# Cosine attention and a hard-swish feed-forward on one core: a new hand-written order of all engines' work, first products that may be issued in two pieces, and other blocks of zero products early on

## The chip, the cores and the metric

The program runs on one core of one Trainium2 chip. The time is the device time of one launch, in microseconds (us), and smaller is better. The kernel before the change took 399.28 us (median of three runs, 398.77 to 400.17).

A core has a matrix engine (TensorE; PE in the profile, its weight loads are PEld), three engines for elementwise work (VectorE is DVE, ScalarE is ACT, GpSimd is POOL), and a queue engine (SyncE, SP) that does nothing here but issue DMA transfers. Each engine takes its instructions strictly in program order and waits, where it must, for semaphores that other engines set.

## The reference

```python
q_n = q / (norm(q, axis=-1) + 1e-06)              # q, k, v: 8 x 12 x 448 x 64
k_n = k / (norm(k, axis=-1) + 1e-06)
attn = softmax(q_n @ k_n.T / tau)                 # tau = 0.1
x = (attn @ v).transpose(0, 2, 1, 3).reshape(8 * 448, 768)
h = x @ w_in                                      # 768 x 2048
g = h * clip(h + 3.0, 0.0, 6.0) / 6.0
out = g @ w_out                                   # 2048 x 768
```

## The kernel before

Heads are worked on in pairs: 8 batches of 12 heads make 48 "items" `i`, six to a batch. Query and key come in as separate loads, so that `j` counts 0 to 47 over them: `j` = 2d and 2d + 1 are query and key of items 2d and 2d + 1.

All engines' order comes from one list of short words, `PLAN` (lines 19 to 117), that `run` (near the end of the file) reads from left to right. Each word issues the instructions of one step, and each engine gets its instructions in the order in which their words stand there. Nothing is rearranged later. The words that matter here:

- `LQ.j` loads 448 KB of query or key through SP's queue (line 262), `LV.d` loads values (line 271). `SQ.j.e.c.n` squares columns c to c + n on engine e (a is ACT, line 296; v is DVE and p is POOL, line 298). `RE.j` sums them (DVE, line 310). `NO.d` makes the reciprocal norms for two j, four short ACT instructions (lines 326 to 329). `NM.j.e` multiplies (line 341); a last number means one of the two heads only.
- `TR.j.Y` or `TR.j.Z` transposes on PE (line 398), for the first 14 j; after them `XD.j` does it by a DMA on SP's queue (line 409). `CQ.i`, `CK.i` and `CS.i` copy the transposed pieces out of PSUM (lines 418 and 420).
- `SC.i.g` is the scores of item i in four groups g (PE, lines 499 and 502), `EX.i.g` their exponentials (ACT, line 521), `VC.i` casts the values (lines 361 and 363), `VA.i.g` multiplies by them into the accumulator `PV` (PE, line 537), `FI.i` divides by the sum (DVE, lines 557 and 558). `BK.i` and `CX.i` transpose the result back into `xT` and copy it (line 575, line 420); `XB` and `XP` do so by DMA.
- `F.b.c` is one first product of batch b, six matmuls over the six chunks of `xT` (PE, line 671); `FA` and `FV` are its two activation steps (ACT line 680, DVE line 686). It needs the results of all six items of its batch. `G` and `P` are the sums and products of the second matrix (line 812, line 837), `BO`, `RS`, `PE.` their combination.
- `W.n` is one of ten weight loads, issued by POOL (line 1131). `DP.n` issues n products of zeros on PE (line 1142) into a part of `PV` that nobody reads; their zeros are `xT` of the second batch, set by DVE at line 1185.

For the first six items the scores go through two PSUM buffers `SC`, and `SC.i.g` waits until the exponentials two groups back have read its buffer. The word `OPEN` ends that: from item 6 on, the same memory is four of the six banks of one ring (M in the profile, with Y and Z), which scores, transposes, first and second products share in turn.

In the list before, the early `DP` blocks have 23, 16, 4, 3, 4, 2, 1 and 3 products, in that order; the first stands ahead of `TR.0`, the second ahead of `TR.1`, the one of 1 after `FI.0`, the last one between `FI.4` and `VA.5.0`.

Of the kernel before, what the change touches and what calls it, by code (L numbers as in the profile page):

```python
# [120 lines left out]
def kernel(  # L121
# [11 lines left out]
    B, H, S, D = q.shape  # L133
# [3 lines left out]
    HP = H // 2  # L137
# [498 lines left out]
    def g_of(b):  # L636
        return gT[b % 2]
# [17 lines left out]
    def g_left(b, e="v"):  # L655
# [3 lines left out]
        engines[e].tensor_copy(out=g_of(b + 1)[:, :, 0:SR], in_=g_of(b)[:, :, S - SR : S])  # L659
        left_done.add(b)  # L660

    def mm1_unit(b, fc):
        needs(*(("CX", i) for i in range(b * HP, (b + 1) * HP)))
        assert all({2 * n, 2 * n + 1} <= weights_in for n, c in enumerate(FF) if c <= 128 * fc)
        assert not any(x in "34" for x, _ in in_summed)
# [569 lines left out]
```

## Time and profile before

| | |
|---|---|
| time, median of three | 399.28 us (398.77 to 400.17) |
| profiled execution, its own time | 401.33 us |
| its span, first to last instruction | 399.5 us |
| mean granted TensorE clock | 0.989 |
| transfers | 64.87 MB, mean 162 GB/s |
| zero products | 56, 10.0 us of PE |

The span is that of one profiled execution. In a row of a timeline stand the start, the time that the instructions of the row took together, the engine, the line, the operation, out and in tiles, and how many; in brackets the idle time ahead of it and what ended it. A row of a window table has, for a stretch of the span, its length, each engine's busy time and count, the granted clock of PE (1.00 is full), and the DMA engines' share and rate. The busy share of the engines in forty equal slices shows at once that PE is full from the fourth slice on:

```profile
PE   4988999999999999999999999999999999999995
ACT  6896999989966888896756876888687567844420
PEclk9898999999999999999999999999999999999999
```

### The profile page before, as it was taken

To read this page: it belongs to the slowest core of one execution; us is meant where nothing else is said; L and a number is where in the kernel's file an instruction comes from. 1 tells how busy PE (TensorE), PEld (TensorE's weight loads), DVE (VectorE), ACT (ScalarE), POOL (GpSimd) and SP (SyncE) were. 2 spreads that over 40 slices of the span, in tenths; PEclk is the share of its full clock that TensorE was granted. 3 is DMA by queue.
4 is the path that set the end of the run, shared out by engine and by line. 5 is a ranking of instruction groups with operands and counts; after the bars stand their busy time and mean duration, and the time that the engine had idled before them with its cause. 6 is when DMAs were issued, how large, how long until landed. Compare 5 with 4: busy or idle time off the path is not lost.

```text
span 399.5 us, 10001 instructions
## 1 busy us (share of the span) xinstructions
PE 385.0 (96%) x3776; PEld 240.9 (60%) x3776; DVE 309.4 (77%) x545; ACT 295.6 (74%) x670; POOL 299.0 (75%) x269
## 2 busy tenths in 40 slices
PE   4988999999999999999999999999999999999995
PEld 3655556545655556655555556655666679977763
DVE  6797877998969698687766968854878868987862
ACT  6896999989966888896756876888687567844420
POOL 4999886799679946477838693778798989675752
PEclk9898999999999999999999999999999999999999
DMA  8979989997899987895996598765466350012124
GB/s 292 309 220 250 208 201 276 185 157 154 206 205 236 194 189 178 192 229 166 200 191 152 140 218 169 194 148 132 107 139 123 82 119 14 2 40 61 40 60 118
DMA packets 90239, 64.87 MB, mean 162 GB/s; under 512 B 55760, under 2 KB 89424, under 8 KB 90192
## 3 DMA queue, kind: packets, MB, share of 16 engines
q1 hardware_dynamic: 85280, 57.56, 59.3%
q0 software_dynamic: 4512, 6.29, 9.3%
q8 instruction: 29, 0.48, 0.5%
q10 hardware_dynamic: 400, 0.39, 0.3%
q14 instruction: 18, 0.15, 0.1%
HBM read 46.73 MB, written 11.01 MB: 145 GB/s over the span
## 4 chain that ended last, share of the span: by engine, by line
PE 81%; POOL 6%; ACT 3%; DVE 3%; DMA 3%; issue 2%; SPq 0%; POOLq 0%; DVEq 0%; ACTq 0%
PE M L837 16%; PE M L671 16%; PE PV L537 10%; PE V L837 6%; PE M L1026 6%; PE M L502 5%; PE Y L671 4%; PE Y L837 4%; PE Z L837 3%; PE Z L671 3%; DMA big<-in_k_dram 2%; POOL nrm L341 2%; ACT att L521 2%; PE Y L502 2%; PE Z L502 1%
## 5 line engine op out<-in xcount | busy, mean ns | idle before, releaser
L521 ACT ACTIVATE att<-M 128x448 bf16<-128x448 f32 x193 | 95.7, 560 | 14.7 <-PE M L502 13.1
L671 PE MATMUL M<-xT,w_in_sb 128*128 128x448 bf16 x396 | 82.9, 353 | 0.0
L671 PEld LDWEIGHTS <-w_in_sb 128*128 128x128 bf16 x576 | 53.1, 98 | 46.8 <-issue 3.4
L341 POOL TENSOR_TENSOR nrm<-big,r 128x896 bf16<-128x896 f32 (+1 forms) x36 | 61.7, 1720 | 16.6 <-ACT r L329 13.0
L537 PEld LDWEIGHTS <-att 128*128 128x128 bf16 (+1 forms) x1536 | 56.3, 97 | 22.7 <-issue 9.9
L537 PE MATMUL PV<-vx,att 128*128 128x65 bf16 (+1 forms) x1536 | 64.9, 194 | 0.0
L837 PEld LDWEIGHTS <-gT 128*128 128x128 bf16 x448 | 42.9, 98 | 28.7 <-POOL gT L812 1.4
L686 DVE SCALAR_TENSOR_TENSOR gT<-u,M 128x448 bf16<-128x448 bf16 x66 | 39.5, 616 | 18.6 <-ACT u L680 18.3
L310 DVE TENSOR_REDUCE n<-big 128x14 f32<-128x896 f32 (+1 forms) x50 | 51.5, 1042 | 1.6 <-ACT big L296 1.3
L680 ACT ACTIVATE u<-M 128x448 bf16<-128x448 f32 x66 | 35.8, 555 | 10.8 <-PE M L671 9.7
L298 POOL TENSOR_TENSOR big<-big 128x896 f32<-128x896 f32 (+2 forms) x19 | 31.5, 1657 | 13.2 <-DMA big<-in_k_dram 6.5
L837 PE MATMUL M<-w_out_sb,gT 128*128 128x384 bf16 x224 | 40.4, 326 | 0.7 <-POOL gT L812 0.7
L837 PEld LDWEIGHTS <-gs 128*128 128x128 bf16 x296 | 28.1, 98 | 18.8 <-issue 1.3
L812 POOL TENSOR_TENSOR gT<-gT 128x1024 bf16<-128x1024 bf16 x15 | 31.9, 2125 | 9.5 <-DVE gs L812 9.0
L558 DVE TENSOR_TENSOR on<-PV,rc 128x512 bf16<-128x512 f32 x48 | 33.2, 691 | 1.6
L837 PE MATMUL M<-w_sum,gs 128*128 128x384 bf16 (+1 forms) x192 | 34.0, 323 | 0.0
L502 PE MATMUL M<-tT,kz 64*128 64x448 bf16 (+1 forms) x171 | 33.4, 356 | 0.6 <-DVE gT L686 0.4
L868 POOL TENSOR_TENSOR big<-big 128x384 f32<-128x384 f32 x14 | 18.3, 1308 | 17.8 <-ACT big L625 15.0
L812 POOL TENSOR_TENSOR gs<-gT 128x1024 bf16<-128x1024 bf16 x14 | 29.7, 2126 | 2.3 <-DVE gT L686 1.2
L521 ACT ACTIVATE att<-Z 128x448 bf16<-128x448 f32 x51 | 28.5, 558 | 1.3 <-PE M L502 1.0
L521 ACT ACTIVATE att<-Y 128x448 bf16<-128x448 f32 x50 | 28.0, 560 | 1.5 <-PE Z L502 1.5
L458 POOL COPY km<-tT 64x128 bf16<-64x128 bf16 x34 | 16.4, 484 | 12.5 <-PE Y L502 5.1
(146 smaller groups left out, 758.9 us busy)
## 6 DMA issues: line engine op xcount, KB each, us to landing
big<-in_q_dram SPq DMA_DIRECT2D x24, 448.0 KB, 4.4
big<-in_k_dram SPq DMA_DIRECT2D x24, 448.0 KB, 4.4
out_dram<-o SPq DMA_DIRECT2D x107, 96.0 KB, 2.2
big<-in_v_dram SPq DMA_DIRECT2D x68, 128.0 KB, 3.2
big<-in_v_dram SPq DMA_DIRECT2D x7, 448.0 KB, 7.0
w_out_sb<-in_moe_w_out_dram POOLq DMA_DIRECT2D x4, 768.0 KB, 10.0
w_in_sb<-in_moe_w_in_dram POOLq DMA_DIRECT2D x4, 384.0 KB, 5.3
w_in_sb<-in_moe_w_in_dram POOLq DMA_DIRECT2D x2, 768.0 KB, 8.4
```

The costliest lines, as they stand in the source:

```text
L298: engines[e].tensor_tensor(out=o, in0=i, in1=i, op=ALU.mult)
L310: nc.vector.tensor_reduce(out=n2s[d % 2][:, j % 2, c], in_=sq[:, :, :, :].rearrange("p g c d -> p (g c) d")[:, c, :], axis=AX.X, op=ALU.add,)
L341: engines[e].tensor_tensor(out=nrm[:, :, g, :].rearrange("p c g d -> p g c d"), in0=raw_of[j][:, g, :, :], in1=rs[d % 2][3][:, j % 2, :] . ...
L502: nc.tensor.matmul(o, ks, qt[rows], start=True, stop=True)
L521: nc.scalar.activation(out=o, in_=x, func=AF.Exp, scale=inv_tau)
L537: nc.tensor.matmul(pv_out(j, h), at[rows, n, q_cols(i // HP, j)], vt[rows, 3 + h if name == "M" else 5 * h + int(name[1]), :], start=(name ...
L558: nc.vector.tensor_tensor(out=on[:, :, :, :].rearrange("p j h d -> p h j d"), in0=pv4[:, :, :, 0:D], in1=rc[:, :, :].to_broadcast([128, 2, ...
L671: nc.tensor.matmul(ps[:, 0:S], w_in_sb[:, cc, fc * 128 : (fc + 1) * 128], x[:, cc, 0:S], start=(cc == 0), stop=(cc == CC - 1),)
L680: nc.scalar.activation(out=u[:, :], in_=ps[:, 0:S], func=AF.Relu, bias=0.5, scale=1.0 / 6.0)
L686: nc.vector.scalar_tensor_tensor(out=g[:, fc, c0 : c0 + S], in0=u[:, :], scalar=1.0, in1=ps[:, 0:S], op0=ALU.min, op1=ALU.mult,)
L812: engines[e].tensor_tensor(out=o[:, :, :], in0=x, in1=y, op=op)
L837: nc.tensor.matmul(m, lhs[:, c, :], rhs[:, c, c0 : c0 + width], start=(base is None and c == 0), stop=(c == KC - 1), skip_group_check=True,)
```

## The change

Three things change; the arithmetic is the same, and each kind of instruction but the zero products keeps its count.

First, `PLAN` is another list, 1902 words for 1899. No block of it is the same for long: the order differs on every engine. Some of the words that name an engine name another one now; on balance ACT gets four squares more, POOL six casts of values more and ACT and DVE three fewer each, DVE both halves of the weight sum `IS.6` from POOL, and four copies of second products from ACT. Its first line in the list before and now:

```diff
-    "LQ.0 SQ.0.v.6.2 SQ.0.a.0.6 RE.0.0 SQ.0.a.8.6 RE.0.1 LQ.1 SQ.1.p.0.4 SQ.1.a.4.3 RE.1.0 SQ.1.v.11.3 SQ.1.a.7.4 RE.1.1 LQ.2 NO.0.0 SQ.2.a.0.7 LQ.3",
+    "LQ.0 SQ.0.a.6.2 SQ.0.a.8.6 SQ.0.v.0.6 RE.0.0 RE.0.1 NO.0.0 LQ.1 SQ.1.a.7.4 SQ.1.v.11.3 RE.1.1 SQ.1.a.4.3 SQ.1.p.0.4 RE.1.0 NM.0.v.1 LQ.2 SQ.2.a.0.7",
```

Second, the early zero blocks are 31, 16, 3, 7, 3, 8, 1 and 3 products, 72 in all. The first two stand ahead of `TR.0` and `TR.1` as before, the one of 1 after `FI.0`; the block between `FI.4` and `VA.5.0` is gone, and the last block of 3 stands ahead of `SC.2.1.1`.

Third, a first product can be issued in two pieces, and the list has three such, `FP.0.3.4`, `FP.0.2.4` and `FP.0.1.4` (the first four chunks), each with its `F.0.c` (the other two) some words later. All three stand behind `CX.5`, the copy of the last chunk of that batch.

```diff
-    def mm1_unit(b, fc):
-        needs(*(("CX", i) for i in range(b * HP, (b + 1) * HP)))
+    part_of = {}
+
+    def mm1_chunks(b, fc, ps, chunks):
+        needs(*(("CX", b * HP + cc) for cc in chunks))
...
+        for cc in chunks:
             nc.tensor.matmul(
                 ps[:, 0:S],
                 w_in_sb[:, cc, fc * 128 : (fc + 1) * 128],
-                x[:, cc, 0:S],
+                xT[b % 2][:, cc, 0:S],
                 start=(cc == 0),
                 stop=(cc == CC - 1),
             )
+
+    def mm1_part(b, fc, n):
+        ps, key = bank_of(None, 1)
+        narrow.discard(key)
+        mm1_chunks(b, fc, ps, range(n))
+        part_of[(b, fc)] = ps, key, n
+
+    def mm1_unit(b, fc):
+        firsts_read.add((b, fc))
+        g, c0 = g_of(b), b % 2 * SR
+        if (b, fc) in part_of:
+            ps, key, n = part_of.pop((b, fc))
+        else:
+            (ps, key), n = bank_of(None, 1), 0
+            narrow.discard(key)
+        mm1_chunks(b, fc, ps, range(n, CC))
```

What moves is seen at three places. On ACT, from the first square to the second group of norms (L296 are squares, L326 to L329 the four instructions of `NO`), it was

```order
L296 ACTIVATE big_87<-big_87 128x384 x2
L296 ACTIVATE big_87<-big_87 128x192
L296 ACTIVATE big_87<-big_87 128x256
L326 ACTIVATE ln0_94<-n20_92 128x14
L327 ACTIVATE nr0_95<-ln0_94 128x14
L328 ACTIVATE le0_96<-nr0_95 128x14
L329 ACTIVATE r0_97<-le0_96 128x14
L296 ACTIVATE big_87<-big_87 128x896
L326 ACTIVATE ln0_94<-n20_92 128x14
```

and now is

```order
L296 ACTIVATE big_87<-big_87 128x128
L296 ACTIVATE big_87<-big_87 128x384
L326 ACTIVATE ln0_94<-n20_92 128x14
L327 ACTIVATE nr0_95<-ln0_94 128x14
L328 ACTIVATE le0_96<-nr0_95 128x14
L329 ACTIVATE r0_97<-le0_96 128x14
L296 ACTIVATE big_87<-big_87 128x256
L296 ACTIVATE big_87<-big_87 128x192
L296 ACTIVATE big_87<-big_87 128x896
L326 ACTIVATE ln0_94<-n20_92 128x14
```

ACT's two squares of the first key load (192 and 256 wide) have moved behind the first group of norms; what ACT no longer squares of the first query load, DVE does.

On DVE, after the second and third sums of squares (`CK.0` is the first row of the first list, `FI.0` its L557 and L558), it was

```order
L420 COPY kz0_80<-Y_107 128x448
L310 TENSOR_REDUCE n20_92<-big_87 128x14 x2
L420 COPY kz1_81<-Y_107 128x448
L341 TENSOR_TENSOR nrm0_89<-big_87,r1_101 128x2x7x64
L361 TENSOR_REDUCE vx_88<-big_87 64x8x64 x2
L298 TENSOR_TENSOR big_87<-big_87 128x896
L420 COPY tT2_85<-Z_108 128x448
L557 RECIPROCAL rc_331<-PV_106 128x8
L558 TENSOR_TENSOR on_330<-PV_106,rc_331 128x2x4x64
L420 COPY kz0_80<-Y_107 128x448
L310 TENSOR_REDUCE n21_93<-big_87 128x14
```

and now is

```order
L420 COPY tT1_84<-Z_108 128x448 x2
L420 COPY kz0_80<-Y_107 128x448
L310 TENSOR_REDUCE n20_92<-big_87 128x14
L420 COPY kz1_81<-Y_107 128x448
L310 TENSOR_REDUCE n20_92<-big_87 128x14
L341 TENSOR_TENSOR nrm0_89<-big_87,r1_101 128x2x7x64
L298 TENSOR_TENSOR big_87<-big_87 128x896
L420 COPY tT2_85<-Z_108 128x448
L310 TENSOR_REDUCE n21_93<-big_87 128x14
L361 TENSOR_REDUCE vx_88<-big_87 64x8x64 x2
L420 COPY kz0_80<-Y_107 128x448
L557 RECIPROCAL rc_351<-PV_106 128x8
```

The two query copies are new on DVE (they were ACT's), and `RE.7` (the L310 that writes n21) and `CK.2` (the second copy into kz0) have moved ahead of `FI.0`.

On SP, where the DMA transposes begin (L262 are loads of query or key, L409 the transposes `XD`, L281 and L271 loads of values, L610 a transpose of results), it was

```order
L262 DMA big_87<-in_k_dram 128x2x448 x2
L262 DMA big_87<-in_q_dram 128x2x448 x2
L262 DMA big_87<-in_k_dram 128x2x448
L281 DMA big_87<-in_v_dram 64x2x256 x4
L409 DMA_TRANSPOSE tT2_85<-nrm0_89 128x7x128
L409 DMA_TRANSPOSE tT0_83<-nrm2_91 128x7x128
L262 DMA big_87<-in_q_dram 128x2x448
L409 DMA_TRANSPOSE tT0_83<-nrm1_90 128x7x128
```

and now is

```order
L409 DMA_TRANSPOSE tT0_83<-nrm2_91 128x7x128
L262 DMA big_87<-in_q_dram 128x2x448
L409 DMA_TRANSPOSE tT2_85<-nrm0_89 128x7x128
L409 DMA_TRANSPOSE tT0_83<-nrm1_90 128x7x128
L409 DMA_TRANSPOSE tT1_84<-nrm2_91 128x7x128
L262 DMA big_87<-in_k_dram 128x2x448
L610 DMA_TRANSPOSE xT0_69<-on_1463 128x8x128
```

The load `LQ.20`, second of the two loads in the first row before, now is the last but one row: it has moved behind the four transposes `XD.14` to `XD.17`.

More of the change, by code (lines that the diff above doesn't have):

```diff
@@ L660, in g_left @@
         left_done.add(b)
-    def mm1_unit(b, fc):
-        needs(*(("CX", i) for i in range(b * HP, (b + 1) * HP)))
+    part_of = {}
+    def mm1_chunks(b, fc, ps, chunks):
+        needs(*(("CX", b * HP + cc) for cc in chunks))
         assert all({2 * n, 2 * n + 1} <= weights_in for n, c in enumerate(FF) if c <= 128 * fc)
         assert not any(x in "34" for x, _ in in_summed)
-        firsts_read.add((b, fc))
-        x, g, c0 = xT[b % 2], g_of(b), b % 2 * SR
-        ps, key = bank_of(None, 1)
-        narrow.discard(key)
-        for cc in range(CC):
+        for cc in chunks:
             nc.tensor.matmul(
@@ L1160 @@
         "GL": g_left, "WS": lambda x, *h: weight_sums(str(x), *((h[0] * KC // 2, KC // 2) if h else (0, KC))), "D": busy, "DP": busy_pv, "OPEN": open_ring,
-        "F": mm1_unit, "S": single_unit, "G": lambda x, n, e="v": g_sum(n, str(x), e), "P": product, "TB": tail_banks, "WR": wide_ring,
+        "F": mm1_unit, "FP": mm1_part, "S": single_unit, "G": lambda x, n, e="v": g_sum(n, str(x), e), "P": product, "TB": tail_banks, "WR": wide_ring,
         "IS": lambda x, e, *n: in_sum(str(x), e, *n), "XS": lambda b, x, *e: x_sum(b, str(x), *e), "QA": quad_first, "QB": quad_second, "QC": quad_third,
```

192 rows, old and new, of the table PLAN are left out of this document.

## The prediction

> **What bounds the kernel now.** I read the page's shares first, then the span in windows, then PE's waits, then the timeline of the first 40 us.
>
> ```profile
> PE 385.0 (96%) x3776; PEld 240.9 (60%) x3776; DVE 309.4 (77%) x545; ACT 295.6 (74%) x670; POOL 299.0 (75%) x269
> PE 81%; POOL 6%; ACT 3%; DVE 3%; DMA 3%; issue 2%; SPq 0%; POOLq 0%; DVEq 0%; ACTq 0%
> ```
>
> PE is busy 385.0 of 399.5 us and makes 81% of the chain that ended last. The share hides that the limits differ by stage, so I cut the span where the work changes: at the first zero product, the first transpose, the first exponential, the end of the fourth group of norms, the first first-product, and the last product.
>
> ```profile
> 2.50:9.18 6.68, 3.92 (x23) 2.87 (x24) 4.15 (x10) 4.17 (x14) 1.74 (x10) 0.96 1.03 384
> 9.18:14.10 4.92, 4.85 (x38) 3.67 (x38) 2.78 (x4) 3.30 (x8) 4.68 (x4) 0.71 1.06 381
> 14.10:35.86 21.76, 18.23 (x274) 12.01 (x273) 20.54 (x41) 20.92 (x37) 21.09 (x21) 1.00 0.89 218
> 35.86:42.56 6.70, 6.57 (x95) 4.42 (x95) 4.33 (x13) 4.11 (x10) 6.59 (x7) 0.75 0.98 351
> 42.56:395.60 353.04, 351.43 (x3350) 217.98 (x3348) 275.82 (x474) 261.85 (x603) 262.99 (x222) 1.00 0.67 150
> ```
>
> From 42.56 us on, PE is busy 351.43 of 353.04 us at full clock: 1.61 us of idle in nine tenths of the program. The list does not change what PE multiplies there, so that stage gets shorter by at most 1.61 us, and can get longer by any new wait. Up to 42.56 us PE is fed by others: from 14.10 to 35.86 ACT is busy 20.92 of 21.76 us, so ACT sets the pace, and before that a chain of loads, squares and norms does. So the question is when PE fills for good, now at 42.56 us, and whether it stays full.
>
> ```profile
> PE Z L398 <- DVE nrm L341: 2.7, 1, 2.7
> PE PV L1142 <- DVE on L558: 1.8, 2, 1.1
> PE M L837 <- POOL gT L812: 0.7, 1, 0.7
> ```
>
> PE's waits agree: 2.7 us ahead of `TR.0`, 1.8 us where zero products wait for `FI`, and one of 0.7 us late.
>
> **Up to the first exponential.** The rows of the chain:
>
> ```profile
> 4.55 0.94 ACT L296 ACTIVATE big<-big 128x384 f32<-128x384 f32 x2 [2.52 <-DMA big<-in_q_dram]
> 5.75 0.67 ACT L296 ACTIVATE big<-big 128x192 f32<-128x192 f32 x2 [0.27 <-DMA big<-in_k_dram]
> 6.33 0.20 ACT L326 ACTIVATE ln<-n 128x14 f32<-128x14 f32 x1
> 6.45 0.62 DVE L310 TENSOR_REDUCE n<-big 128x7 f32<-128x448 f32 x1 [0.20 <-ACT big L296]
> 7.17 0.93 ACT L296 ACTIVATE big<-big 128x896 f32<-128x896 f32 x1
> 8.09 0.21 ACT L326 ACTIVATE ln<-n 128x14 f32<-128x14 f32 x1
> 7.98 1.15 DVE L341 TENSOR_TENSOR nrm<-big,r 128x448 bf16<-128x448 f32 x2
> 9.04 2.07 DVE L310 TENSOR_REDUCE n<-big 128x14 f32<-128x896 f32 x2
> 9.12 1.84 POOL L341 TENSOR_TENSOR nrm<-big,r 128x448 bf16<-128x448 f32 x2 [2.70 <-ACT r L329]
> 9.18 0.93 PE L398 MATMUL Z<-ident,nrm 128*128 128x128 bf16 x7 [2.75 <-DVE nrm L341]
> 9.90 2.92 PE L1142 MATMUL PV<-xT 128*128 128x248 bf16 x16
> 12.66 0.55 PE L398 MATMUL Y<-ident,nrm 128*128 128x128 bf16 x7
> 13.05 0.59 PE L1142 MATMUL PV<-xT 128*128 128x248 bf16 x4
> 13.25 0.39 DVE L420 COPY kz<-Y 128x448 bf16<-128x448 bf16 x1 [2.14 <-PE Y L398]
> 14.10 2.97 ACT L521 ACTIVATE att<-SC 128x896 bf16<-128x896 f32 x4 [1.26 <-PE SC L502]
> ```
>
> The two parts of the first query's squares are dealt out the other way, and the sums still begin near 5.1 us; the first norms stay at 6.33 to 7.26. Behind them ACT now squares its part of the first key load (0.67 us, before done from 5.75), so `RE.1.1` starts at 7.6, `RE.1.0` ends at 8.8 (0.6 us each), and DVE's half of `NM.0` (1.15 / 2), queued behind both, ends at 9.35. `TR.0` starts at 9.4 instead of 9.18. POOL's half, 0.92 us from 7.3, lies beside. The second norms start at 8.85 instead of 8.09, `NM.1` on POOL ends at 11.7 instead of 10.96.
>
> Before, that slack of `NM.1` was worth nothing, because 16 zero products stood between the two transposes at half clock: 2.92 us. At full clock the block of 4 shows about 0.11 us apart, so 16 take 1.7. `TR.0` 9.4 to 9.95, zeros to 11.65, `TR.1` 11.75 to 12.3, if the clock holds. On DVE, `RE.2` and `RE.3` now end near 11.9 (`SQ.3` on ACT ends at 10.75 behind the norms), the two query copies at 12.65, `CK.0` at 13.05. In the old trace the first exponential follows the start of `CK.0` by 0.85 us; less its 0.39 us, that is 0.45 behind its end: 13.5. So it comes 0.6 us earlier. The eight more zeros of the first block (0.11 to 0.17 us each) end at 7.4, inside the 2.75 us of idle: they cost nothing up to that gap's length.
>
> **The clock.** Whether it holds is the largest doubt here:
>
> ```profile
> 5.24:8.65 3.41, 1.20 (x11) 0.86 (x9) 3.10 (x7) 2.98 (x11) 0.61 (x1) 1.00 1.04 387
> 8.67:12.06 3.39, 2.88 (x18) 2.32 (x19) 2.44 (x3) 3.03 (x8) 2.70 (x3) 0.50 1.06 382
> 32.56:35.95 3.39, 1.91 (x24) 1.20 (x21) 2.40 (x9) 2.79 (x7) 3.20 (x4) 1.00 0.98 191
> 35.97:39.37 3.40, 3.38 (x40) 2.32 (x40) 1.51 (x7) 0.98 (x2) 3.40 (x3) 0.50 1.03 361
> ```
>
> Twice a stretch of 3.4 us at half clock follows one in which PE was busy 1.20 and 1.91 us. The changed first block leaves PE idle from 7.4 to 9.4, 2.0 us, so a stretch that holds all of it has 1.4 us of work: between the two. If it halves again, `TR.1` is at 13.2 and the first exponential at 14.65. The Trainium skill ("TensorE: Matmul & The Clock Gate", "Part 1: The HAM clock gate") says that such stretches run free, so that their phase differs from run to run, and that at least one idle stretch throttles. The trace doesn't agree with the second: after 1.91 us of work in 3.39 the clock was already halved. By that rule of the Trainium skill alone no gap of 2.0 us could halve the clock, and rival 1 below would fall away.
>
> **From the first exponential to the ring.**
>
> ```profile
> 18.24 1.36 DVE L298 TENSOR_TENSOR big<-big 128x896 f32<-128x896 f32 x1
> 20.06 0.69 DVE L558 TENSOR_TENSOR on<-PV,rc 128x512 bf16<-128x512 f32 x1
> 20.67 0.38 DVE L420 COPY kz<-Y 128x448 bf16<-128x448 bf16 x1
> 20.96 1.08 DVE L310 TENSOR_REDUCE n<-big 128x14 f32<-128x896 f32 x1
> 21.16 3.41 ACT L521 ACTIVATE att<-SC 128x448 bf16<-128x448 f32 x5
> 35.63 0.23 ACT L329 ACTIVATE r<-le 128x28 f32<-128x28 f32 x1
> 35.99 0.78 PE L1142 MATMUL PV<-xT 128*128 128x248 bf16 x3 [1.12 <-DVE on L558]
> 38.16 0.98 ACT L521 ACTIVATE att<-M 128x448 bf16<-128x448 f32 x2 [2.30 <-PE M L502]
> ```
>
> The zero product behind `FI.0` still stands ahead of `SC.2.0.0`, and `FI.0` is now queued behind `RE.7` and `CK.2` on DVE. From the end of `CK.0` (13.6) to that of `FI.0` (20.75) DVE took 7.15 us; with 1.0 and 0.3 more, and from 13.05, it is 21.5. `EX.2.0` can start near 22.05. ACT would be ready at 13.5 + 7.6 = 21.1 (before, 14.10 to 21.70 with the same instructions): a new gap of 1.0 us, and 0.35 us behind the old trace. Bounds: 0, if DVE's queue runs closer, and 1.3, all that was put ahead of `FI.0`.
>
> From there ACT did 13.8 us of work up to 35.86, the end of `NO.4`, and then idled 2.30 us for the first scores of the ring. The list puts `NO.4` ahead of `EX.5.2`, so that gap is filled: ACT has the same 13.8 us, plus some 0.6 us of small gaps where a score stands behind `VA` on PE (0 to 1.2), and reaches the ring at 36.45. `SC.6.0` needs only the buffer that `EX.5.2` frees 0.55 us earlier, and the copies of `TR.7`, which PE now does near 35. So `EX.6.0` comes near 36.5 instead of 38.16: 1.65 us earlier. Of that, the zero block behind `FI.4`, gone with its wait of 1.1 us, and the half clock from 35.97 are what made the old ring late; what is late next is `FI.5`. `VA.6.2` (0.25 us) now stands behind the first first-products, so 1.4 us remain when PE fills.
>
> The other zeros (7 and 8, 1.7 us) stand ahead of scores that wait for ACT's 0.8 us exponentials; without that cover they'd cost those 1.7 us. The `FP` pieces add no matmul and each stands behind the copy of the last chunk, so their early start is never used: zero. The last products are the same, and so is the end.
>
> **The full stage.** I take the old 1.6 us of waits, bounds 0 and 4.5. Below: PE cannot idle less than nothing. Above: POOL's longest wait for a load, where a square is placed close behind its load, is
>
> ```profile
> 205.53 1.68 POOL L298 TENSOR_TENSOR big<-big 128x896 f32<-128x896 f32 x1 [4.24 <-DMA big<-in_k_dram]
> big<-in_k_dram SPq DMA_DIRECT2D x24, 448.0 KB, 4.4
> 42.63 1.24 PE M L671 x6
> ```
>
> 4.24 us, of which 0.7 us reached PE. I take the middle of nothing new, since 0.7 is the nearest thing that this stage has shown.
>
> **The sum.** 399.5 - 1.4 = 398.1 us of span. The profiled execution took 401.33 us in its own count and the median is 399.28; I carry the difference over: 399.28 - 1.4 = 397.9 us.
>
> **Rivals.** (1) *The gain is eaten at the start.* The clock halves at `TR.0` again: the first exponential at 14.65 shifts DVE's queue and all behind it by 1.15 us, leaving 0.25: 399.0 us. For it, the row with 1.20 us; against it, eight more zeros.
>
> (2) *Slower: ACT stands still at `SQ.20`.* `LQ.20` is now behind `XD.17` on SP, and `SQ.20` is on ACT as the next word, with `EX.16.1` and the activations of two first-products behind. `XD.17` waits for `SC.13.3`. Between that and `SQ.20` PE has six first-products (1.14 us apart), nine score groups (0.2) and eight value groups (0.3), some 11 us, against 4.4 us for the load and the issue of transposes. That speaks against it. If the transposes hold SP back until PE has reached `SC.16.0`, ACT waits 4.4 us more; PE covers two first-products of it, 2.3, and idles 2.1 us, and as much again where DVE and the ring follow late: 4.2 - 1.4 = 2.8 us slower, 402.1, or 400.5 with the first wait alone and the start's gain lost by half. I say 401. It decides from a landing over 2.3 us behind `SQ.20`'s turn.
>
> (3) *More than hoped.* `FI.0` is in time and the late waits go: 397.9 - 1.0 - 0.7 = 396.2.
>
> **How the numbers follow.** Forecast 0.48, rival 1 0.21, rival 2 with other new waits of PE in the full stage 0.24, rival 3 0.07. A measurement here tells about 0.3%, 1.2 us, from no change: faster is below 398.1, slower above 400.5. The forecast's own range, 396.9 to 399.3, gives 0.37 faster, 0.08 same, 0.03 slower; rival 1 gives 0.02, 0.14 and 0.05; rival 2 is slower, rival 3 faster. Together 0.46, 0.22 and 0.32. The range reaches from rival 3 to rival 2: 396.0 to 401.3; it leaves out the ends at which two bounds come together.
>
> **What would show it.** Right: PE's clock stays at full from 5 us on, the first exponential near 13.5, an ACT gap of about 1 us near 21 ended by a score, no gap of 2.3 us ahead of the first exponential out of M, the first first-product near 41, PE idle some 1.6 us from there on. Wrong: a window at 0.50 behind the first zero block (rival 1); a wait of ACT for a load by L296 near 90 us, or waits of PE over 3 us behind 42 us (rival 2). If the first first-product comes early and the time doesn't, the new order lost it in the full stage.

## The result and the profile after

The changed kernel takes 401.27 us (median of 20 runs, 399.08 to 403.49), the kernel before, run beside it, 398.95 us (20 runs, 397.44 to 400.80). The ratio is 1.0062, with a 95% interval of 1.0046 to 1.0077: slower by 2.3 us, where 1.4 us less were predicted. The two profiled executions lie only 1.1 us apart in span, because the one of before was a long one: 401.33 us, 2.4 above the median of its kernel, against 1.2 for the changed kernel's.

The profiled execution of the changed kernel took 402.48 us, its span is 400.6 us. First the page: busy time by engine, the chain that ended last by engine, and PE's busy tenths and clock in forty slices.

```profile
PE 385.8 (96%) x3792; PEld 243.4 (61%) x3792; DVE 308.8 (77%) x547; ACT 293.2 (73%) x663; POOL 295.5 (74%) x274
PE 83%; DVE 6%; ACT 5%; DMA 3%; POOL 2%; issue 1%; SPq 0%; ACTq 0%; DVEq 0%; POOLq 0%
PE   5887999999999999999999999999999999999995
PEclk9988999999999999999999999999999999999999
```

Little differs: PE is busy 0.8 us longer, with 16 more zero products. But in the chain DVE has 6% for 3% before, and PE's fourth slice (30 to 40 us) now shows 7 tenths. It showed 8 before, where PE was full from the fifth slice on. The windows say the same in numbers (columns as in the prediction's window table). The first two rows are the start, the last runs from the first first-product to where PE's work thins out at the end.

```profile
14.00:36.00 22.00, 18.23 (x235) 11.44 (x234) 19.23 (x32) 19.10 (x31) 19.89 (x20) 0.92 0.92 225
36.00:43.00 7.00, 6.30 (x95) 4.42 (x95) 5.68 (x17) 4.05 (x10) 5.68 (x5) 0.76 0.84 277
45.29:396.60 351.31, 350.55 (x3358) 219.62 (x3356) 272.44 (x474) 260.25 (x598) 259.87 (x228) 1.00 0.69 150
```

Behind the first first-product PE idles 0.76 us in 351.31, against 1.61 in the row of before: the long stage is better by 0.85 us. Ahead of it ACT, which set the pace with 20.92 of 21.76 us, is busy 19.10 of 22.00 us, and the first first-product starts at 45.29 instead of 42.56 us. From there on 355.3 us of the span remain instead of 356.9; of the difference 0.85 is idle time, the rest PE's work that now stands ahead of that point. So the start lost 2.7 us and the rest gave 1.6 back. Where the start lost them, in order of time (rows of the timelines of ACT, DVE, PE and POOL):

```profile
13.98 2.53 ACT L521 ACTIVATE att<-SC 128x896 bf16<-128x896 f32 x3 [0.43 <-PE SC L502]
21.43 0.69 DVE L558 TENSOR_TENSOR on<-PV,rc 128x512 bf16<-128x512 f32 x1
22.18 0.27 PE L1157 MATMUL PV<-xT 128*128 128x248 bf16 x1 [1.17 <-DVE on L558]
22.78 0.92 ACT L521 ACTIVATE att<-SC 128x896 bf16<-128x896 f32 x1 [1.19 <-PE SC L502]
26.24 0.21 DVE L557 RECIPROCAL rc<-PV 128x8 f32<-128x8 f32 x1 [2.53 <-PE PV L537]
27.88 0.23 ACT L329 ACTIVATE r<-le 128x28 f32<-128x28 f32 x1
28.24 1.69 POOL L341 TENSOR_TENSOR nrm<-big,r 128x896 bf16<-128x896 f32 x1 [0.97 <-POOL vx L363]
29.87 1.35 POOL L1146 DMA_DIRECT2D w_in_sb<-in_moe_w_in_dram  x2
30.90 2.99 DVE L298 TENSOR_TENSOR big<-big 128x896 f32<-128x896 f32 x1
31.23 1.71 POOL L341 TENSOR_TENSOR nrm<-big,r 128x896 bf16<-128x896 f32 x1
35.63 0.69 DVE L558 TENSOR_TENSOR on<-PV,rc 128x512 bf16<-128x512 f32 x1
36.38 0.60 PE L537 MATMUL PV<-vx,att 128*128 128x65 bf16 x8 [1.77 <-DVE on L558]
37.35 0.23 ACT L326 ACTIVATE ln<-n 128x28 f32<-128x28 f32 x1 [1.37 <-DVE n L310]
41.19 0.98 ACT L521 ACTIVATE att<-M 128x448 bf16<-128x448 f32 x2 [0.81 <-PE M L502]
45.29 0.93 PE L669 MATMUL M<-xT,w_in_sb 128*128 128x448 bf16 x4
```

`FI.0` (21.43) holds back a zero product, the score behind it and `EX.2.0`: a gap of 1.19 us, as the prediction had it. Then comes what it did not have: `SQ.9` on DVE (L298) takes 2.99 us. In the profile of before it took 1.08, begun as far into the same two weight loads of POOL (1.05 us for 1.03), with a cast of values behind them instead of `NM.7`:

```profile
28.08 1.35 POOL L1131 DMA_DIRECT2D w_in_sb<-in_moe_w_in_dram  x2
29.13 1.08 DVE L298 TENSOR_TENSOR big<-big 128x896 f32<-128x896 f32 x1
29.42 1.93 POOL L363 CAST vx<-big 64x512 bf16<-64x512 f32 x2
```

In the changed kernel `FI.3` is queued behind the square and ends at 36.32; PE stands still for 1.77 us and ACT for 1.37. And the clock halves twice, behind each of the two waits. In the windows below PE was busy 2.00 and 1.44 of 3.41 us just ahead of each stretch at 0.50.

```profile
19.24:22.65 3.41, 2.00 (x37) 1.29 (x36) 3.33 (x8) 2.35 (x4) 3.14 (x5) 1.00 1.17 191
22.65:26.06 3.41, 3.41 (x41) 2.04 (x39) 1.06 (x2) 2.63 (x3) 3.35 (x3) 0.50 0.72 186
32.89:36.30 3.41, 1.44 (x20) 0.77 (x17) 3.38 (x7) 3.02 (x5) 2.71 (x4) 1.00 1.16 185
36.30:39.70 3.40, 3.32 (x43) 2.44 (x43) 2.61 (x6) 1.58 (x5) 2.22 (x2) 0.50 1.03 374
```

The 20 runs show what the clock costs. A stretch of 3.4 us at half clock lowers the mean granted clock by 0.0043 (1.7 of 400 us). The three runs at 1.000 took 399.08 to 400.16 us, the seven at 0.994 to 0.996 400.08 to 401.50, the eight at 0.990 and 0.991 401.23 to 402.48, the two at 0.986 402.70 and 403.49. By the medians of these groups each stretch goes with some 1.1 to 1.4 us, and the median run has one or two.

### The profile page after: what moved, and what is told of

The parts are those of the page before. It is cut to its first block, busy times and chain, and to the rows that moved or that the text cites. A ratio compares the mean times of both kernels' runs of the same rounds, so it can differ in the third digit from the quotient of the medians.

```text
span 400.6 us, 10046 instructions
## 1 busy us (share of the span) xinstructions
PE 385.8 (96%) x3792; PEld 243.4 (61%) x3792; DVE 308.8 (77%) x547; ACT 293.2 (73%) x663; POOL 295.5 (74%) x274
## 4 chain that ended last, share of the span: by engine, by line
PE 83%; DVE 6%; ACT 5%; DMA 3%; POOL 2%; issue 1%; SPq 0%; ACTq 0%; DVEq 0%; POOLq 0%
PE M L669 16%; PE M L852 16%; PE PV L537 10%; PE V L852 6%; PE Z L852 6%; PE M L1041 6%; PE M L502 5%; PE Y L669 4%; PE Y L852 4%; PE Z L669 3%; ACT att L521 2%; DMA big<-in_q_dram 2%; PE Z L502 2%; PE Y L502 1%; PE Y L1041 1%; PE Z L1041 1%
## 5 line engine op out<-in xcount | busy, mean ns | idle before, releaser
L521 ACT ACTIVATE att<-M 128x448 bf16<-128x448 f32 x202 | 100.6, 558 | 17.2 <-PE M L502 15.5
L669 PE MATMUL M<-xT,w_in_sb 128*128 128x448 bf16 x372 | 78.1, 353 | 0.0
L341 POOL TENSOR_TENSOR nrm<-big,r 128x896 bf16<-128x896 f32 (+1 forms) x38 | 63.4, 1669 | 15.8 <-ACT r L329 13.8
L310 DVE TENSOR_REDUCE n<-big 128x14 f32<-128x896 f32 (+1 forms) x50 | 51.6, 1041 | 9.3 <-ACT big L296 6.0
L852 PE MATMUL M<-w_out_sb,gT 128*128 128x384 bf16 x208 | 37.9, 326 | 0.0
L827 POOL TENSOR_TENSOR gs<-gT 128x1024 bf16<-128x1024 bf16 x15 | 32.2, 2154 | 5.8 <-issue 3.3
L558 DVE TENSOR_TENSOR on<-PV,rc 128x512 bf16<-128x512 f32 x48 | 33.2, 691 | 1.7
L827 POOL TENSOR_TENSOR gT<-gT 128x1024 bf16<-128x1024 bf16 x13 | 29.3, 2256 | 5.1 <-DVE gs L827 3.6
L852 PE MATMUL M<-w_sum,gs 128*128 128x384 bf16 (+1 forms) x176 | 31.2, 322 | 0.0
L298 POOL TENSOR_TENSOR big<-big 128x896 f32<-128x896 f32 (+2 forms) x16 | 26.3, 1648 | 5.9 <-DMA big<-in_k_dram 2.1
L296 ACT ACTIVATE big<-big 128x896 f32<-128x896 f32 (+4 forms) x29 | 25.2, 882 | 5.5 <-DMA big<-in_q_dram 3.4
L883 POOL TENSOR_TENSOR big<-big 128x384 f32<-128x384 f32 x14 | 16.4, 1174 | 16.2 <-DVE big L627 13.5
L521 ACT ACTIVATE att<-Z 128x448 bf16<-128x448 f32 x47 | 26.3, 560 | 2.0 <-PE M L502 1.9
```

Source lines behind the costliest of these rows:

```text
L310: nc.vector.tensor_reduce(out=n2s[d % 2][:, j % 2, c], in_=sq[:, :, :, :].rearrange("p g c d -> p (g c) d")[:, c, :], axis=AX.X, op=ALU.add,)
L341: engines[e].tensor_tensor(out=nrm[:, :, g, :].rearrange("p c g d -> p g c d"), in0=raw_of[j][:, g, :, :], in1=rs[d % 2][3][:, j % 2, :] . ...
L521: nc.scalar.activation(out=o, in_=x, func=AF.Exp, scale=inv_tau)
L558: nc.vector.tensor_tensor(out=on[:, :, :, :].rearrange("p j h d -> p h j d"), in0=pv4[:, :, :, 0:D], in1=rc[:, :, :].to_broadcast([128, 2, ...
L669: nc.tensor.matmul(ps[:, 0:S], w_in_sb[:, cc, fc * 128 : (fc + 1) * 128], xT[b % 2][:, cc, 0:S], start=(cc == 0), stop=(cc == CC - 1),)
L827: engines[e].tensor_tensor(out=o[:, :, :], in0=x, in1=y, op=op)
```

## The experiments

Theory A: the loss is in the start, from `FI.0` on, and the long stage gains. Rivals: B, the loss is in the long stage; C, the zero blocks or the FP pieces; D, only where the half-clock stretches fall. The table has all runs: median, range, ratio to the runs of before on the same chip with its interval (their medians there were 398.83 to 399.04), and from each profile the first exponential, `SQ.9`'s duration, the first exponential out of the ring (`EX.6.0`), the first first-product and the span (us).

| run | median (range) | ratio [95%] | first exp. | SQ.9 | ring | first product | span |
|---|---|---|---|---|---|---|---|
| before | 398.95 (397.44–400.80) | 1 | 14.10 | 1.08 | 38.16 | 42.56 | 399.5 |
| the change | 401.27 (399.08–403.49) | 1.0062 [1.0046, 1.0077] | 13.98 | 2.99 | 41.19 | 45.29 | 400.6 |
| h1 old start, new rest | 397.91 (396.33–399.86) | 0.9967 [0.9941, 0.9994] | 12.48 | 1.14 | 35.62 | 39.52 | 394.6 |
| h2 new start, old rest | 402.72 (401.59–405.15) | 1.0094 [1.0057, 1.0132] | 12.98 | 3.47 | 39.34 | 43.70 | 402.9 |
| e1 VC.2 behind FI.0 | 396.57 (396.44–396.79) | 0.9935 [0.9910, 0.9959] | 13.10 | 1.08 | 35.55 | 39.47 | 394.7 |
| e7 RE.7 behind FI.0 | 396.39 (396.28–397.53) | 0.9956 [0.9939, 0.9972] | 13.04 | 1.08 | 35.38 | 39.31 | 394.5 |
| e2 SQ.9 early | 398.30 (398.15–399.16) | 0.9987 [0.9968, 1.0006] | 13.22 | 1.60 | 37.41 | 41.33 | 396.5 |
| a3 NM.7 ahead of W.2, W.1 | 397.79 (397.70–399.59) | 0.9986 [0.9969, 1.0004] | 12.96 | 2.09 | 36.51 | 40.60 | 395.8 |
| c1 e1 and a3 together | 398.44 (397.85–399.61) | 0.9989 [0.9971, 1.0008] | 14.06 | 1.08 | 36.52 | 40.74 | 397.5 |
| f2 e1 without FP | 396.48 (396.42–397.30) | 0.9944 [0.9924, 0.9963] | 12.97 | 1.08 | 35.42 | 39.34 | 394.6 |
| z3 e1, first block 23 | 397.47 (396.44–398.46) | 0.9967 [0.9948, 0.9986] | 15.38 | 1.08 | 37.42 | 41.34 | 396.6 |
| z1 before, first block 31 | 397.46 (397.37–400.47) | 0.9973 [0.9954, 0.9991] | 12.45 | 1.13 | 35.58 | 39.48 | 395.6 |
| zh1 h1, first block 31 | 397.44 (396.37–397.99) | 0.9959 [0.9940, 0.9978] | 13.58 | 1.18 | 36.78 | 40.68 | 395.8 |
| e4 e1, W.0, W.3 behind VC.0 | 397.06 (396.89–401.25) | 0.9983 [0.9956, 1.0010] | 13.00 | 1.28 | 35.93 | 39.85 | 395.1 |
| e5 e1, W.0, W.3 behind VC.1 | 396.98 (396.90–397.88) | 0.9962 [0.9948, 0.9977] | 13.08 | 1.55 | 36.01 | 39.93 | 395.2 |
| n1 e1, old first loads | 395.85 (395.77–396.05) | 0.9935 [0.9913, 0.9958] | 12.44 | 1.08 | 34.82 | 38.74 | 393.9 |
| n2 change, old first loads | 401.04 (399.73–403.43) | 1.0065 [1.0041, 1.0088] | 13.96 | 3.46 | 40.30 | 44.00 | 399.2 |

One column pair carries the whole study. In every kernel with the new rest but c1, the span is the start of the first first-product plus 355.1 to 355.3 us, the change itself among them (400.6 - 45.29 = 355.3). With the old rest it is 356.1 (z1), 356.9 (before) and 359.2 (h2, where the seam costs). What differs from kernel to kernel is when the first first-product starts. Where a load of the first phase landed late in the profiled run (the change, c1, n2, zh1: ACT's square of the third load waited 1.0 to 1.7 us for it), the first exponential is about 1 us late as well, so single profiles differ by that much, and medians decide.

### Start and rest exchanged (h1, h2)

The diff is the list itself: the words of one up to `SC.7.2`, the words of the other behind it.

> The list before up to the word SC.7.2 (the last one ahead of the first first-product), then the new list's words in the new order. Theory A (the start loses, the full stage gains): the first first-product comes near 42.6 us as before, PE idles about 0.7 us from there on against 1.6 us, so some 0.9 us less than before: near 398. Theory B (the loss is in the full stage): near the changed kernel's time, 401. Theory D (only the phase of the half-clock stretches): between, 399 to 401.

> The new list up to SC.7.2, then the list before in its own order. Theory A: the first first-product near 45.3 us, PE's idle time behind it 1.6 us as before: the slowest of all, near 402. Theory B: near 399, as before. Theory D: 399 to 401.

h1 took 397.91 us, h2 402.72. A holds in both, B falls: the new rest under the old start is the faster kernel, the new start under the old rest the slowest of all. In h2 the seam costs as well: besides 2.3 us for a `FI` PE waits 2.0 us for DVE at 50.95 us, and the clock halves behind that wait.

### One word of DVE's queue behind FI.0 (e1, e7)

```diff
-RE.7 LV.1 VC.2.v CK.2.v VA.0.0 VA.0.3 VA.0.2 VA.0.1 FI.0 EX.1.1
+RE.7 LV.1 CK.2.v VA.0.0 VA.0.3 VA.0.2 VA.0.1 FI.0 VC.2.v EX.1.1
```

> The new list with one word moved: VC.2.v, DVE's cast of values, stands behind FI.0 instead of ahead of it. Theory A: FI.0 starts some 0.6 us earlier (21.43 to about 20.8), the zero product behind it and EX.2.0 as well; 0.3 to 0.6 us less than the changed kernel if nothing later swallows it, about 400.8. Rivals (full stage, or the clock's phase): no change, 401.3.

e7 leaves `VC.2.v` and moves `RE.7` instead:

```diff
-RE.7 LV.1 VC.2.v CK.2.v VA.0.0 VA.0.3 VA.0.2 VA.0.1 FI.0 EX.1.1
+LV.1 VC.2.v CK.2.v VA.0.0 VA.0.3 VA.0.2 VA.0.1 FI.0 RE.7 EX.1.1
```

> The changed kernel with one word moved: RE.7, the sum of squares that the prediction named (1.07 us on DVE), stands behind FI.0; VC.2.v stays ahead of it. If a late FI.0 starts the loss, whatever it is late behind: FI.0 starts near 20.7 us, about 396.6 to 397.5, as where VC.2.v was moved. If it is VC.2's own place that counts: 401.3.

396.57 and 396.39 us: either word takes away 4.7 to 4.9 us, where 0.3 to 0.6 were expected of e1. So it is `FI.0`'s lateness, not either word's place. The rows of e1 show what follows from it (timelines of ACT, DVE, POOL and PE):

```profile
13.10 2.54 ACT L521 ACTIVATE att<-SC 128x896 bf16<-128x896 f32 x3 [0.43 <-PE SC L502]
20.10 0.69 DVE L558 TENSOR_TENSOR on<-PV,rc 128x512 bf16<-128x512 f32 x1
21.45 2.99 ACT L521 ACTIVATE att<-SC 128x896 bf16<-128x896 f32 x4 [0.73 <-PE SC L502]
26.66 1.69 POOL L341 TENSOR_TENSOR nrm<-big,r 128x896 bf16<-128x896 f32 x1
28.29 1.35 POOL L1146 DMA_DIRECT2D w_in_sb<-in_moe_w_in_dram  x2
28.30 1.08 DVE L298 TENSOR_TENSOR big<-big 128x896 f32<-128x896 f32 x1
29.64 1.71 POOL L341 TENSOR_TENSOR nrm<-big,r 128x896 bf16<-128x896 f32 x1
31.11 0.69 DVE L558 TENSOR_TENSOR on<-PV,rc 128x512 bf16<-128x512 f32 x1
35.55 0.98 ACT L521 ACTIVATE att<-M 128x448 bf16<-128x448 f32 x2
```

From the first exponential to `FI.0` it is 7.00 us here and 7.45 in the changed kernel: only 0.45 us. What counts is where `SQ.9` then stands against POOL. Between `NM.6` and `NM.7` POOL issues two weight loads, 1.35 us. In e1 `SQ.9` starts 0.01 us into them and is done before `NM.7`; in the changed kernel it starts 1.03 us into them, and ends only 0.95 us after `NM.7`.

Both engines are late in the changed kernel's profile, but not by the same amount. Counted from the first exponential, `SQ.9` comes 1.72 us later than in e1 and `NM.7` 0.71 us later. DVE waits 2.53 us ahead of `FI.1` for value products that PE does in the stretch at half clock; POOL waits 0.97 us ahead of `NM.6`, and not for its own cast, done at 27.27, that the row names, but for the norms `NO.3` (ACT's L329, done at 28.11), which stand behind the exponentials. The half clock is not needed for the meeting: in h2 and n2 the clock is full up to there, `SQ.9` comes 0.34 us later than in e1 and `NM.7` 0.20 us earlier, and `SQ.9` takes 3.47 and 3.46 us. The rows of n2 (DVE and POOL):

```profile
29.50 3.46 DVE L298 TENSOR_TENSOR big<-big 128x896 f32<-128x896 f32 x1
30.30 1.71 POOL L341 TENSOR_TENSOR nrm<-big,r 128x896 bf16<-128x896 f32 x1
```

In the changed kernel `FI.3` then comes 4.52 us later than in e1 (0.88 of it from the first exponential), and the clock halves behind each of the two waits. All seven runs of e1 and all twelve of e7 have a mean clock of at least 0.998; only three of the changed kernel's twenty do.

### SQ.9 against NM.7 (e2, a3, c1)

e2 moves the square itself:

```diff
-VA.1.2 VA.1.1 FI.1 EX.2.2 LQ.9 SC.2.3.1
+VA.1.2 VA.1.1 LQ.9 SQ.9.v.0.7 RE.9 FI.1 EX.2.2 SC.2.3.1
...
-NM.6.p SC.4.0.0 SQ.9.v.0.7 TR.6.Y
+NM.6.p SC.4.0.0 TR.6.Y
...
-CQ.6.v RE.9 VA.3.2
+CQ.6.v VA.3.2
```

> The new list with LQ.9, SQ.9.v and RE.9 moved ahead of FI.1, into the stretch from 23.7 to 26.2 us in which DVE stood idle. Theory A: FI.3 is no longer queued behind that square (2.99 us) and its sum, PE's wait of 1.77 us near 36.4 and ACT's of 1.37 us near 37.4 go, the first first-product comes near 43.3 instead of 45.3: about 399.3. The square itself should take about 1.1 us, as POOL's products with two inputs no longer lie beside it. Rivals: no change, 401.3.

398.30 us, 3.0 less than the changed kernel; the square took 1.60 us instead of the 1.1 expected, since at 22.87 it met another product of POOL (to 23.53). The wait behind `FI.0` stays, and in e2's profile so does a stretch at half clock behind it (21.91 to 25.32 us): the 3.0 us come from the second wait and the half clock behind it.

a3 leaves DVE's and PE's lists alone and changes POOL's:

```diff
-TR.6.Y EX.4.0 W.2 CQ.7.v
+TR.6.Y EX.4.0 CQ.7.v
...
-VA.3.3 BK.2.Z W.1 SC.4.2.0
+VA.3.3 BK.2.Z SC.4.2.0
...
-FI.4 NM.7.p TR.7.Z
+FI.4 NM.7.p W.2 W.1 TR.7.Z
```

> The changed kernel with POOL's weight loads W.2 and W.1 behind NM.7 instead of ahead of it; DVE's and PE's lists untouched. In the changed kernel NM.7 ran from 31.23 to 32.94 us and SQ.9 on DVE, begun at 30.90, ended only at 33.89. If a two-input product of POOL and a two-input square of DVE shut each other out (the one that comes second waits for the first): NM.7 runs near 29.9 to 31.6, SQ.9 ends near 32.6 instead of 33.89, FI.3 1.2 us earlier, about 400.0, and some 1 us less if a half-clock stretch goes with it. Rival (the loss sits in FI.0 alone): 401.3.

397.79 us, 3.5 less than the changed kernel and 2.2 below the expected 400.0, by the order of three words on an engine that is busy 74% of the time. Its profile has no stretch at half clock. `NM.6` and `NM.7` now run back to back, and `SQ.9`, begun at 28.50, ends 0.94 us behind them:

```profile
26.32 3.33 POOL L341 TENSOR_TENSOR nrm<-big,r 128x896 bf16<-128x896 f32 x2
28.50 2.09 DVE L298 TENSOR_TENSOR big<-big 128x896 f32<-128x896 f32 x1
```

c1 makes the same swap in e1, meant to bring the collision back:

> The list of the run in which VC.2.v stands behind FI.0 (396.57 us), with one more move: POOL's weight loads W.2 and W.1 go behind NM.7, so that NM.7, a product with two inputs on POOL, should begin near 28.3 us, just when DVE squares the tenth load (SQ.9, 1.08 us there). DVE's list and PE's are untouched. If a two-input product of POOL makes DVE's two-input square stand still: SQ.9 takes 2.5 to 3.0 us again, FI.3 ends 1.5 to 1.9 us later, PE and ACT wait for it, 1 to 3 us more: about 398.5. Rival (SQ.9 was long in the changed kernel for another reason): SQ.9 stays near 1.1 us and the time at 396.6.

The time came out as expected, 398.44, but not for that reason. `SQ.9` kept its 1.08 us; this time POOL lost: its two products took 4.26 us, 0.88 more than 2 x 1.69. And PE's time went to a wait for the weights, which the swap had made late:

```profile
27.62 4.26 POOL L341 TENSOR_TENSOR nrm<-big,r 128x896 bf16<-128x896 f32 x2
29.26 1.08 DVE L298 TENSOR_TENSOR big<-big 128x896 f32<-128x896 f32 x1
43.45 0.92 PE L669 MATMUL M<-xT,w_in_sb 128*128 128x448 bf16 x4 [1.41 <-DMA w_in_sb<-in_moe_w_in_dram]
```

So in none of these profiles do the two run side by side, and either can be the one that waits. The same swap gains 3.5 us in one list and loses 1.9 in another.

### The zero blocks and the pieces (z1, z3, zh1, f2)

```diff
-DP.23 TR.0.Z
+DP.31 TR.0.Z
```

> The kernel before with 31 products in the first block of zeros instead of 23, nothing else. If the longer block keeps the clock full at the first transposes: no half-clock stretch near 8 to 12 us, mean clock of more runs at 0.998 to 1.0, median 0.5 to 1 us lower: about 398.2. Rival (the early zeros change nothing): 399.0.

397.46 us: by the medians, eight more zeros alone are worth 1.5 us to the kernel before; the ratio says 1.1 (0.4 to 1.8). In its profile, with a mean clock of 1.0, no stretch is at half clock, where before had two. The windows at those places:

```profile
8.60:12.10 3.50, 3.13 (x36) 2.71 (x38) 2.74 (x5) 3.41 (x9) 3.01 (x3) 1.00 1.06 380
36.00:39.40 3.40, 3.40 (x59) 2.16 (x58) 3.06 (x7) 3.40 (x9) 3.40 (x3) 1.00 1.02 344
```

And the timeline of ACT, at the first exponential and at the first one out of the ring:

```profile
12.45 2.97 ACT L521 ACTIVATE att<-SC 128x896 bf16<-128x896 f32 x4 [0.16 <-PE SC L502]
35.58 0.98 ACT L521 ACTIVATE att<-M 128x448 bf16<-128x448 f32 x2 [1.42 <-PE M L502]
```

```diff
-NM.0.p.0 DP.31 TR.0.Z
+NM.0.p.0 DP.23 TR.0.Z
```

> The list of the run in which VC.2.v stands behind FI.0, with 23 products in the first block of zeros as before the change instead of 31. If the longer block is what keeps the clock full at the first transposes (rival 1 of the prediction the other way round): some runs have one half-clock stretch more, mean clock 0.994 to 0.996, 0.5 to 1 us longer, about 397.3. Rival (the number of zeros does nothing): 396.6.

The reverse in e1: 397.47 us, 0.9 more, ten of twelve runs at 0.994 to 0.998.

zh1 is h1 with the edit of z1:

> The run with the old start and the new rest (397.91 us, 396.33 to 399.86), with 31 products in the first block instead of 23. If the block holds the clock: most runs near 396.4, median about 396.6. Rival: 397.9 again with the same spread.

In zh1 the clock is at least 0.998 in all twelve runs, and the highest time falls from 399.86 to 397.99; but only five runs are near 396.4 to 396.8, the others 397.3 to 398.0, and the median, 397.44, is within the spread of h1. The block holds the clock there too; the rest of the spread is not the clock's. In the profile the first exponential is 1.1 us later than h1's, at full clock, because ACT's square of the third load waited 1.30 us for it; whether the other long runs have the same cause is not shown.

f2 takes the three FP words from e1, of which the first is

```diff
-FP.0.3.4 SC.7.3 EX.7.2 EX.7.3 F.0.3
+SC.7.3 EX.7.2 EX.7.3 F.0.3
```

> The list of the run in which VC.2.v stands behind FI.0, without the three FP words: the same first products, each issued whole at the place of its second piece. Forecast: no change, 396.6 (within 0.3). If pieces filled a gap of PE: up to 3 x 0.8 us longer.

396.48 us against 396.57: the FP pieces do nothing, as predicted. C falls with these runs: the pieces are nothing, the longer block is a gain, and the other blocks stand in e1 as in the change.

### What else could be had (e4, e5)

e4 moves two weight loads behind `VC.0`; e5 puts them behind `VC.1.p`:

```diff
-NM.2.p W.0 W.3 DP.7
+NM.2.p DP.7
...
-NO.2 VC.0.p NM.3.v
+NO.2 VC.0.p W.0 W.3 NM.3.v
```

> The list of the run in which VC.2.v stands behind FI.0, with POOL's weight loads W.0 and W.3 (1.51 us of POOL) behind VC.0 instead of ahead of it. There FI.0 waited 0.86 us for the first value products, and these for VC.0, which ended near 18.5 us. Theory A (the path to the ring runs through FI.0): VC.0 ends near 16.5, FI.0 starts 0.8 us earlier, ACT's gap of 0.73 us ahead of EX.2.0 goes: about 395.9. Rival (ACT or the load queue sets the end): 396.6.

> The list of the run in which VC.2.v stands behind FI.0 (396.57 us), with POOL's weight loads W.0 and W.3 behind VC.1. In the run that put them behind VC.0 alone (397.06) ACT's gap ahead of EX.2.0 shrank from 0.73 to 0.33 us, but VC.1 came late and a gap of 0.58 us opened behind it. With both casts ahead of the loads the two gaps should go: 0.5 us less than 396.57, about 396.1. Rival (the weights now land late for the first first-products, as in the run with W.2 and W.1 moved): 397 to 398.

Both missed: 397.06 and 396.98 us. Counted from the first exponential `FI.0` comes 0.4 us earlier, half of what was meant, but `SQ.9` now overlaps `NM.6` (1.28 and 1.55 us for 1.08), in e4 `FI.2` is late by 0.3 us too, and the ring starts at 35.93 and 36.01 instead of 35.55.

### The order of the first loads (n1, n2)

In both the words up to `EX.0.0` are those of before, with its first block at 31; they begin

```diff
-LQ.0 SQ.0.a.6.2 SQ.0.a.8.6 SQ.0.v.0.6 RE.0.0 RE.0.1 NO.0.0 LQ.1
+LQ.0 SQ.0.v.6.2 SQ.0.a.0.6 RE.0.0 SQ.0.a.8.6 RE.0.1 LQ.1
...
```

n1 has the rest of e1, n2 that of the changed kernel.

> The list of the run in which VC.2.v stands behind FI.0 (396.57 us), but up to the first exponential in the order before (squares, sums, norms and transposes of the first loads, with the first zero block at 31). In runs at full clock the first exponential came at 12.5 us with the old order of the first loads and at 13.0 to 13.1 with the new one. If that order is a cost of its own: first exponential near 12.5, the ring near 35.0, about 396.0. Rival (what follows swallows it, since VC.0, the loads or ACT set the pace): 396.6.

> The changed kernel with nothing undone but the order up to the first exponential, which is the one before (with the first zero block at 31). If the new order of the first loads is what made the change slower: near 398.5 or less. If the loss sits behind it (FI.0 late, SQ.9 against NM.7, the clock that halves in the waits), only 0.5 us at most go: 400.5 to 401.3.

n1, 395.85 us (all six runs within 0.3), is the fastest of all, faster than the kernel before by 3 us (2.6 by the ratio). With the old order of the first loads, full clock and no load late the first exponential comes at 12.44 to 12.48 us (h1, z1, n1), with the new one at 12.96 to 13.22 (eight profiles). n2, with `FI.0` still late, gains nothing that can be told: 401.04, and `SQ.9` takes 3.46 us. The new order of the first loads costs 0.5 to 0.7 us, and is not what made the change slower.

## Why the prediction was wrong

The parts now add up, each good to some tenths. From before to e1, by medians: the first block of 31, -1.5 (z1); the new order of the first loads, +0.7 (n1 against e1). By single profiles: the new order of ACT, which reaches the ring 22.45 us behind the first exponential (e1) instead of 23.13 (z1), -0.7; the long stage, -1.0 (spans behind the first first-product, h1 against z1). That is -2.5, and e1 is 2.4 us below before. From e1 to the change, +4.7: `FI.0` late. Of those, some 2.1 are half clock (401.27 against 399.16, the middle one of the three runs at full clock). So D is part of it, but e1 and e7 show that the half-clock stretches go with the waits. The other 2.6 are order; a3, which keeps `FI.0` late and takes away most of the meeting with `NM.7`, is 1.4 us below those full-clock runs and 1.2 above e1.

**The step that failed** is in "From the first exponential to the ring": "ACT has the same 13.8 us, plus some 0.6 us of small gaps where a score stands behind `VA` on PE (0 to 1.2)". From `EX.2.0` to the ring it took 18.41 us (22.78 to 41.19) instead of 14.4. The work was right, 13.93 us; the gaps were 4.1 us, 1.1 of them in and just behind the stretch at half clock that follows `FI.0`, and 2.8 behind `FI.3`. The prediction shifted everything behind `FI.0` by one number and kept each duration of the old rows. DVE and POOL shifted by different amounts, so `SQ.9` moved 1.0 us against `NM.7` (0.5 in h2 and n2), and its 1.08 us became 2.99. "What is late next is `FI.5`" was wrong for the same reason: it was `FI.3`, behind that square.

**What was right.** `FI.0` behind `RE.7`: 8.14 us from the first exponential to its end, 8.0 predicted, and the gap of 1.0 us came out at 1.19. e7 shows the same step in the other direction. `NO.4` ahead of `EX.5.2` fills ACT's gap where `FI.0` is in time: in e1 no idle time stands ahead of the ring. But that gap was sized at 2.30 us on a stretch of half clock; at full clock (z1) it is 1.42. FP worth zero: f2. No wait of ACT for a load near 90 us: rival 2 did not happen; from 45.29 us on the view of PE's waits lists a single one, 0.4 us. That the measured 401.27 us lies just inside the stated range, next to rival 2's 401, is therefore luck. The 400.5 given beside it is a slip: 399.28 + 2.1 - 0.7 is 400.7. The full stage kept less than its 1.6 us of idle time: 0.76.

**The first exponential** was to come at 13.5, 0.6 earlier. It came at 13.98, in a run whose third load was late, and near 13.0 in the others. The 0.6 was the clock's: against an old start at full clock the new order is later, not earlier. The profile of before had two half-clock stretches (399.5 us of span; z1 without them 395.6), and the prediction measured the list against them.

**Rival 1** had the right mechanism at the wrong place. The clock did not halve at `TR.0`, behind the block of 31, though PE stood idle there for 1.94 us as predicted, but at 22.65 and 36.30, behind waits that the prediction itself had made (the first) or not seen (the second). It was given one price of 1.15 us, for one stretch; there were two in the profile, and the price of each was about right.

The Trainium skill ("SBUF — State Buffer", "Who interferes with whom") says that a VectorE instruction with two SBUF inputs contends with a GpSimd instruction that reads SBUF, that the port pair they share is an exclusive lock, and that issue order decides which of them is blocked. The records agree with the exclusion: 2.99, 3.46 and 3.47 us where `SQ.9` lost, 0.88 us more for POOL where it won, 1.08 where they didn't meet. That the first to issue wins, the recorded starts don't bear out (next section but one). The prediction used no such rule, though before already had a row of 1.36 us for the same kind of square (at 18.24, beside casts of values on POOL) among those it quoted.

## What to carry to other kernels

A list in program order is tuned against the times at which engines happen to meet; each engine waits for other steps and shifts by another amount, so a delay of 0.45 us became 2.6 us here, and 4.7 with the clock. Before a row's duration is carried over to a shifted schedule, look what ran beside it on an engine with which it cannot overlap (here POOL, for DVE's two-input squares), and whether the shift brings something else there. And split the trace of before into what the order costs and what the clock cost in that execution: the profiled one took 401.33 us, the fastest of the same kernel 397.3.

## What the runs showed that was not expected

- `SQ.9` began 0.33 us (the change) and 0.80 us (h2, n2) ahead of the recorded start of `NM.7` and still ended 0.95 us behind it. The weight loads issued just ahead on POOL do not hold it back by themselves: in h1, z1 and zh1 it began 0.53 to 0.59 us into the same two loads, as in h2 and n2 (0.55), but as in before with a cast of values behind them instead of `NM.7`, and took 1.13 to 1.18 us. Whether POOL's recorded starts are late was not tried. Where the square began within 0.1 us of the first load's issue (e1, e7, n1, f2, z3) it took 1.08 us beside them.
- Stretches at half clock lie on a grid of 3.41 us: the two of the changed kernel start 13.65 us apart, those of before 27.30. In the windows just ahead of them PE was busy 0.89 to 2.02 us (before, the change, e2, h2, n2); in windows of the same grids with 2.10 to 2.24 us (the change, h2, n2) and more the next one stayed at full clock. The window that holds the end of the first zero block and PE's idle time ahead of `TR.0` does not fit: 1.84 us in the changed kernel (2.02 in n2), and the next one stayed at full clock, with `TR.0` at 0.55 us. Why is open. The rows of the changed kernel:

```profile
5.59:9.00 3.41, 1.84 (x17) 1.45 (x15) 2.35 (x6) 1.65 (x7) 1.55 (x2) 1.00 1.02 377
9.00:12.41 3.41, 2.24 (x23) 1.89 (x23) 2.29 (x3) 3.14 (x7) 1.77 (x2) 1.00 1.06 384
```

- A granted clock of 1.00 in the records is not always full speed: in z3's profile, mean clock 1.0, the first transposes take 0.91 us, where they take 0.55 in the changed kernel, and the first exponential comes 2.3 us later than in e1:

```profile
9.27 0.91 PE L398 MATMUL Z<-ident,nrm 128*128 128x128 bf16 x7 [1.86 <-DVE nrm L341]
```
